# A layer's forward and backward pass on one core: turned weights prepared in the forward chain, loads at both phase changes queued in order of need, and a tail with its small blocks spread

## The chip, the core and the metric

The kernel runs on one core of a Trainium2 chip. The metric is device time in microseconds (us) of one execution; the profile is one execution of the same program under the hardware profiler. TensorE does the matmuls, VectorE and ScalarE empty its accumulators, GpSimd (POOL) copies, clears and issues DMAs, and SyncE (SP) issues DMAs only.

## The reference, cut to what matters

The output is a transformer layer and the gradients of everything in it.

```python
# A: attention with a recurrent memory of M = 8 rows, S = 2048 tokens, segments of 32 -> 64 steps one after another
mem = mem0
for s in range(64):
    h = concat([mem, layernorm(x)[32*s : 32*s+32]])      # 40 rows of D = 448
    q, k, v = h @ Wq, h @ Wk, h @ Wv                     # 16 heads of 256 -> 4096 columns
    o = softmax(mask(q k^T / 16)) v @ Wo
    mem, out[s] = o[:8], o[8:]
h  = x + out
# B: gated feed-forward unit (FFN), F = 1792
h2 = h + (silu(n @ w_gate) * (n @ w_up)) @ w_down        # n = layernorm(h)
# returned: h2 and, for the given gradient of h2, d x, d mem0, d Wq, d Wk, d Wv, d Wo, d w_gate, d w_up, d w_down
```

So there is a forward chain of 64 dependent segments, an FFN phase (forward and backward for 8 units of 256 rows), a backward chain of 64 segments, and a tail that computes all weight gradients.

## The kernel before

Between the phases the weights in on-chip memory are exchanged. The FFN backward needs w_gate, w_up and w_down turned (transposed), and the backward chain needs all four attention weights turned. Before, each is turned by a DMA transpose at the moment of the phase change. A helper does one weight in five DMAs; other weights take one transpose each:

```python
def transposed_rows(k, dst, src2d, tmp):
    for kc in range(3):
        nc.sync.dma_start_transpose(out=dst[:, kc, :], in_=src2d[:, kc * P:(kc + 1) * P])
    nc.sync.dma_start_transpose(out=tmp, in_=src2d[:, k.D - P:k.D])
    nc.sync.dma_start(out=dst[0:64, 3, :], in_=tmp[64:P, :])
    ...
# ffn_phase, one unit of two row tiles (cut)
for gi in range(NT // G):
    for tt in range(G):
        nc.sync.dma_start(out=h_t, in_=dr["Hh"][rows, :])
        nc.vector.tensor_scalar(out=hn_t[:, 0:D], in0=h_t, ...)                       # layernorm
        nc.sync.dma_start_transpose(out=hnT[:, :, tt * P:(tt + 1) * P], in_=hn_t)
        nc.sync.dma_start(out=dout_t[:, 0:D], in_=GO2[rows, :])
        nc.sync.dma_start_transpose(out=doT[:, :, tt * P:(tt + 1) * P], in_=dout_t)
    if gi == 0:
        transposed_rows(k, WdT_sb, Wd2, wdT_tmp)
        nc.gpsimd.dma_start(out=Wd_sb, in_=...)
        nc.sync.dma_start_transpose(out=WgT_sb, in_=Wg2)
        nc.sync.dma_start_transpose(out=WuT_sb, in_=Wu2)
    proj(Wg_sb, hnT, gate)                                                            # L560: the matmuls of proj
    ...                                                                               # L589: VectorE in gate
# backward_chain, ahead of its loop
transposed_rows(k, WoT_sb, k.Wo2, woT_tmp)
...
prep_tile(NT - 1)
load_seg(NSEG - 1)                                     # V, Q, K of the first segment, turned by DMA
for (Wsrc, WT) in ((k.Wk2, WkT_sb), (k.Wv2, WvT_sb), (k.Wq2, WqT_sb)):
    nc.sync.dma_start_transpose(out=WT, in_=Wsrc)      # L706
# one backward segment, the order in which it needs weights: WoT, then
heads("v", ...); rows_in("v", WvT_sb, 0, MC)           # heads: results go to blk[nm]; rows_in: L780
heads("k", ...); rows_in("k", WkT_sb, 0, 20)
heads("q", ...); rows_in("k", WkT_sb, 20, MC); rows_in("q", WqT_sb, 0, MC)
```

In the tail, each half of an attention weight gradient needs 16 row tiles (`X_`, by DMA transpose) and four packed blocks of memory rows (`M_`). The four blocks are loaded, copied and turned one after another through one load buffer and one pack buffer:

```python
def load_m(nm, hf):
    for g in range(NG):
        nc.gpsimd.dma_start(out=ld, in_=dr["M_" + nm]...)
        nc.vector.tensor_copy(out=pk[:, 0:8], in_=ld[...])       # L919
        nc.scalar.copy(out=pk[:, 8:16], in_=ld[...])
        ...
            nc.tensor.transpose(pt[...], pk[...], ident[:, :])   # L925
```

Of the kernel before, what the change touches and what calls it, by code (L numbers as in the profile page):

```python
# [9 lines left out]
FP32 = mybir.dt.float32  # L10
# [26 lines left out]
class _K:  # L37
# [31 lines left out]
    def evac(self, out, in_, eng=None):  # L69
        nc = self.nc  # L70
        if eng is None:
            eng = "v" if (self._evac_i % 2 == 0) else "s"
            self._evac_i += 1
        if eng == "v":
            nc.vector.tensor_copy(out=out, in_=in_)  # L75
        else:
            nc.scalar.copy(out=out, in_=in_)  # L77
# [69 lines left out]
def run_all(k: _K):  # L147
# [67 lines left out]
    for nm in ("q", "k", "v"):  # L215
        dr["X_" + nm] = dt("X_" + nm, [NT, P, MC * P])
        dr["M_" + nm] = dt("M_" + nm, [NT, P, MC * 32])
    k.dr = dr

    forward_chain(k)  # L220
    ffn_phase(k)
    backward_chain(k)
# [12 lines left out]


def transposed_rows(k, dst, src2d, tmp):

    nc = k.nc
    for kc in range(3):  # L240
        nc.sync.dma_start_transpose(out=dst[:, kc, :], in_=src2d[:, kc * P:(kc + 1) * P])
    nc.sync.dma_start_transpose(out=tmp, in_=src2d[:, k.D - P:k.D])
    nc.sync.dma_start(out=dst[0:64, 3, :], in_=tmp[64:P, :])
    nc.gpsimd.memset(dst[64:P, 3, :], 0.0)


def ln_bwd(k, outs, dxn_ap, xn_ap, rstd_col, t1, junk):
# [13 lines left out]
    for out_ap, resid_ap, c0, c1 in outs:  # L261
        nc.vector.scalar_tensor_tensor(out=out_ap, in0=t1[:, c0:c1], scalar=rstd_col, in1=resid_ap, op0=ALU.mult, op1=ALU.add)


def forward_chain(k: _K):
# [125 lines left out]
    def to_token_major(blk, t):  # L391
        for hf in range(2):
            ot = stg()
            nc.sync.dma_start_transpose(out=ot.rearrange("p (a b) -> p a b", b=P),
                                        in_=blk[:, 16 * hf:16 * hf + 16, :].rearrange("p c n -> p (c n)"))
            nc.gpsimd.dma_start(out=dr["X_o"][t][:, hf * 2048:(hf + 1) * 2048], in_=ot)

    for s in range(NSEG):
# [7 lines left out]
        with k.prio.crit():  # L406
            wpass(Wq_sb, s, qT)
            wpass(Wk_sb, s, kT)
            pS = k.ps1()
# [8 lines left out]
            for b in range(4):  # L418
                for kc in range(KC):
                    for g in range(2):  # L420
# [3 lines left out]
                                         start=(kc == 0), stop=(kc == KC - 1), skip_group_check=True)  # L424
            S_sb = k.f32("f2", 8 * L, "S_sb")[:].rearrange("p (h n) -> p h n", n=L)
# [33 lines left out]
            for j in range(MC):  # L459
                nc.tensor.matmul(pO[32 * (j % 4):32 * (j % 4) + M, 0:D], lhsT=o8[:, j, :], rhs=Wo_sb[:, cj(j), :],  # L460
                                 start=(j < 4), stop=(j >= MC - 4), skip_group_check=True)
            for (c0, n, v) in ov:
                k.evac(xblk[:, c0:c0 + n, r * SEG:(r + 1) * SEG], v[:, :, 0:SEG], "svs"[c0 // 12])
# [17 lines left out]
        if (r == 0 and t > 0) or s == 2:  # L481
            prep_tile(t + 2)
        if r == 3:
# [8 lines left out]
            to_token_major(xblk, t)  # L492
        if jm == 15:
            to_token_major(mblk, NT + s // 16)
# [4 lines left out]
            nc.gpsimd.dma_start(out=dr["XN"][r0:r0 + P, :], in_=mrow[:, 0:DP])  # L499


def ffn_phase(k: _K):
# [12 lines left out]
    Wg_sb, Wu_sb = W(0, KC, F), W(14, KC, F)  # L515
    dout_b = [W(28 + i, DP) for i in range(4)]
    WdT_sb, Wd_sb = W(32, KC, F), W(46, FC, D)
    wdT_tmp = W(58.25, F)
    WgT_sb, WuT_sb = W(64, FC, D), W(76.25, FC, D)
    big = [W(96 + 7 * i, G, FC, P) for i in range(4)] + [W(88.5, G, FC, P)] + [A(7 * i, G, FC, P) for i in range(6)]  # L520
    tstg_b = [A(42 + 3.5 * i, FC, P) for i in range(2)] + [W(58.25, FC, P)]
    hnT_b = [A(49 + 2 * i, KC, G * P) for i in range(2)]
    doT_b = [A(53 + 2 * i, KC, G * P) for i in range(2)]
    h_b = [A(57 + 0.875 * i, D) for i in range(4)]
    hn_b = [A(60.5 + i, DP) for i in range(4)]
    o_b = [B(0.875 * i, D) for i in range(2)]
    dhb_b = [B(2 + i, DP) for i in range(2)]
    junk = B(4, D)

    pad_rows(k, Wg_sb, Wg2, nc.gpsimd)  # L530
    pad_rows(k, Wu_sb, Wu2, nc.gpsimd)
    sd = smal.tile([P, NT], FP32, name="sd2", bufs=1)
    nc.scalar.activation(out=sd[:], in_=mv2[:, :, 1], func=ACT.Sqrt, bias=k.eps_t[:], scale=1.0)
    nc.vector.reciprocal(out=rstd2[:], in_=sd[:])
# [3 lines left out]
    for i in range(2):  # L538
        nc.gpsimd.memset(dhb_b[i][:, D:DP], 0.0)

# [7 lines left out]
    def tmajor(src, t, tt, dst):  # L548
        stg = tstg_b[rot[0] % 3]
# [14 lines left out]
    for gi in range(NT // G):  # L564
        hnT, doT = hnT_b[gi % 2], doT_b[gi % 2]
        for tt in range(G):
            t = G * gi + tt
            rows = slice(t * P, (t + 1) * P)
            h_t, hn_t, dout_t = h_b[t % 4], hn_b[t % 4], dout_b[t % 4]
            nc.sync.dma_start(out=h_t, in_=dr["Hh"][rows, :])  # L570
            nc.vector.tensor_scalar(out=hn_t[:, 0:D], in0=h_t, scalar1=mv2[:, t, 0:1], scalar2=rstd2[:, t:t + 1],
                                    op0=ALU.subtract, op1=ALU.mult)
            nc.sync.dma_start_transpose(out=hnT[:, :, tt * P:(tt + 1) * P], in_=hn_t)
            nc.gpsimd.dma_start(out=dr["HN"][rows, :], in_=hn_t[:, 0:D])
            nc.sync.dma_start(out=dout_t[:, 0:D], in_=GO2[rows, :])
            nc.sync.dma_start_transpose(out=doT[:, :, tt * P:(tt + 1) * P], in_=dout_t)
        if gi == 0:
            transposed_rows(k, WdT_sb, Wd2, wdT_tmp)
            nc.gpsimd.dma_start(out=Wd_sb, in_=Wd2.rearrange("(c p) d -> p c d", p=P))
            nc.sync.dma_start_transpose(out=WgT_sb, in_=Wg2)  # L580
            nc.sync.dma_start_transpose(out=WuT_sb, in_=Wu2)

        e = gi % 2
        g, z, t1, dz, u = big[5 + e], big[7 + e], big[9], (big[10], big[4])[e], big[0 + e]
        sg = big[2 + e]
# [15 lines left out]
        proj(Wu_sb, hnT, up)  # L601
        proj(WdT_sb, doT, dzf)
        for tt in range(G):
            t = G * gi + tt
            rows = slice(t * P, (t + 1) * P)
            tmajor(z, t, tt, dr["Zt"])
# [4 lines left out]
            nc.vector.tensor_tensor(out=o_t, in0=pf[:, 0:D], in1=h_b[t % 4], op=ALU.add)  # L611
            nc.gpsimd.dma_start(out=OUT0[rows, :], in_=o_t)
        for tt in range(G):
            nc.vector.tensor_tensor(out=u[:, tt], in0=dz[:, tt], in1=u[:, tt], op=ALU.mult)
            nc.vector.tensor_tensor(out=u[:, tt], in0=u[:, tt], in1=sg[:, tt], op=ALU.mult)
            nc.vector.tensor_tensor(out=g[:, tt], in0=dz[:, tt], in1=g[:, tt], op=ALU.mult)
        for tt in range(G):
            t = G * gi + tt
            rows = slice(t * P, (t + 1) * P)
            tmajor(u, t, tt, dr["DGP"])  # L620
            tmajor(g, t, tt, dr["DU"])
            pdh = k.fx1()
            i = 0
            for (srcT, WT) in ((u, WgT_sb), (g, WuT_sb)):
                for c in range(FC):
                    nc.tensor.matmul(pdh[:, 0:D], lhsT=srcT[:, tt, c, :], rhs=WT[:, c, :], start=(i == 0), stop=(i == 2 * FC - 1))
                    i += 1
            dh_t = k.f32("f3", D, "dh_t")
            t1f = k.f32("f2", D, "t1f")
            ln_bwd(k, [(dh_t[:], dout_b[t % 4][:, 0:D], 0, D)], pdh[:, 0:D], hn_b[t % 4][:, 0:D], rstd2[:, t:t + 1], t1f[:], junk)  # L630
            nc.gpsimd.dma_start(out=dr["DH"][rows, :], in_=dh_t[:])
            dh_b = dhb_b[tt]
            nc.scalar.copy(out=dh_b[:, 0:D], in_=dh_t[:])
# [432 lines left out]
```

## Time and profile before

The time is 3459.89 us (median of 3 runs, 3448.79 to 3468.05). The profiled execution is one of the shorter ones, 3429.5 us; a second profile of the same kernel, taken later, has 3438.8 us.

First the page: busy time of TensorE, then TensorE's busy tenths and its granted clock in 40 slices of 85.7 us.

```profile
PE 3044.6 (89%) x55036; PEld 2058.0 (60%) x55046; DVE 1308.3 (38%) x2912; ACT 971.0 (28%) x2171; POOL 616.2 (18%) x1293
...
PE   5999999999999578882999999999999899999999
...
PEclk8999999999999899995999999999999899999999
```

TensorE is at nine tenths almost everywhere. The slices that are not are the load at the start, the change to the FFN (slices 14 and 15), the FFN, the change to the backward chain (slice 19, with clock 0.5), and slice 32, where the tail begins. That is where time can be won without removing matmuls.

The view of TensorE's waits (what was waited for, sum in us, times, longest) names them:

```profile
PE psf L560 <- DMA arA<-arA: 48.6, 6, 43.7
PE psf L737 <- POOL arA L672: 41.1, 1, 41.1
...
PE psf L560 <- DVE arA L589: 27.8, 7, 7.2
PE po L780 <- DMA arW<-in_A_Wv_dram: 25.5, 1, 25.5
...
PE ph L925 <- DVE arA L919: 15.5, 11, 6.5
PE psf L385 <- issue: 13.1, 16, 2.1
```

The first is the change to the FFN (the first rows come turned), the second and fourth are the change to the backward chain, the third is inside the FFN, the fifth the packed memory blocks of the tail. L385, "issue", is in the forward chain.

The timeline of SyncE's queue (start, duration, what) shows why the two changes are slow: transposes of whole weights stand one behind another in the queue.

```profile
1157.27 12.55 SPq L241 DMA_TRANSPOSE arW<-in_B_w_down_dram  x2
...
1179.62 15.34 SPq L580 DMA_TRANSPOSE arW<-in_B_w_gate_dram  x1
...
1552.21 21.00 SPq L706 DMA_TRANSPOSE arW<-in_A_Wq_dram  x1
...
1587.86 16.90 SPq L706 DMA_TRANSPOSE arW<-in_A_Wk_dram  x1
1604.85 13.64 SPq L706 DMA_TRANSPOSE arW<-in_A_Wv_dram  x1
```

Note that the scheduler issued Wq first, although the program names Wk, Wv, Wq and the segment needs Wv first.

### The profile page before, as it was taken

How to read it: one execution, taken by the hardware profiler on the slowest of the kernel's cores; microseconds unless marked ns; L12 is line 12 of the kernel's file. 1: busy time of each engine (PE TensorE's matmuls, PEld its weight loads, DVE VectorE, ACT ScalarE, POOL GpSimd, SP SyncE). 2: the span in 40 equal slices, each digit the busy share in tenths (PEclk: the TensorE clock that was granted, in tenths of full speed). 3: DMA queues.
4: the chain of work that ended last, by engine and by line, in shares of the span. 5: the costliest groups of instructions: out<-in, count | busy, mean ns of one | idle time of the engine just before them, and what ended most of it. 6: DMA issues, size and time to landing. Idle time of an engine off the chain costs nothing.

```text
span 3429.5 us, 120857 instructions
## 1 busy us (share of the span) xinstructions
PE 3044.6 (89%) x55036; PEld 2058.0 (60%) x55046; DVE 1308.3 (38%) x2912; ACT 971.0 (28%) x2171; POOL 616.2 (18%) x1293
## 2 busy tenths in 40 slices
PE   5999999999999578882999999999999899999999
PEld 4777777777777355661666666666666454443444
DVE  4444444444444256670444444444444201111101
ACT  1333333333333223330333333333333202111100
POOL 2111111111111111111122121212221111111111
PEclk8999999999999899995999999999999899999999
DMA  7545433644544787899688777878787969888571
GB/s 263 155 133 149 155 125 128 174 136 131 148 139 134 196 189 176 185 210 229 142 159 178 164 168 157 177 161 165 166 177 163 308 195 209 175 173 173 155 249 38
DMA packets 994213, 583.65 MB, mean 170 GB/s; under 512 B 904564, under 2 KB 913108, under 8 KB 992100
## 3 DMA queue, kind: packets, MB, share of 16 engines
q1 hardware_dynamic: 925748, 340.37, 47.6%
q0 software_dynamic: 67952, 235.56, 20.6%
q8 instruction: 430, 7.05, 0.9%
q14 instruction: 83, 0.68, 0.1%
HBM read 104.05 MB, written 250.19 MB: 103 GB/s over the span
## 4 chain that ended last, share of the span: by engine, by line
PE 61%; issue 13%; DMA 10%; DVE 8%; SPq 4%; ACT 2%; POOL 2%; ACTq 0%; DVEq 0%; POOLq 0%
PE psf L385 12%; PE po L780 7%; PE psf L422 5%; PE psf L737 5%; PE psf L945 4%; PE psf L715 4%; PE po L460 3%; PE fx L486 3%; PE fx L839 3%; PE psf L560 2%; SPq L910 2%; PE psf L802 2%; DVE arA L75 2%; PE psf L469 2%; DMA arW<-in_A_Wo_dram 2%
## 5 line engine op out<-in xcount | busy, mean ns | idle before, releaser
L77 ACT CAST arA<-psf 128x320 bf16<-128x320 f32 (+4 forms) x1139 | 487.0, 447 | 1611.8 <-PE psf L385 449.5
L75 DVE CAST arA<-psf 128x384 bf16<-128x384 f32 (+6 forms) x1029 | 491.7, 495 | 1085.1 <-PE psf L945 363.3
L385 PE MATMUL psf<-arA,arW 128*128 128x40 bf16 x16384 | 434.9, 181 | 34.3 <-issue 13.1
L385 PEld LDWEIGHTS <-arW 128*128 128x128 bf16 x16384 | 432.7, 97 | 49.6 <-issue 26.9
L780 PE MATMUL po<-arW,arA 128*32 128x448 bf16 x6144 | 355.2, 362 | 46.9 <-DMA arW<-in_A_Wv_dram 25.5
L737 PE MATMUL psf<-arA,arW 128*128 128x40 bf16 x8192 | 219.6, 180 | 51.3 <-POOL arA L672 41.1
L945 PE MATMUL psf<-arW,arA 128*128 128x512 bf16 x990 | 252.7, 383 | 13.4 <-DMA arW<-X_k 7.1
L422 PE MATMUL psf<-arW,arA 128*64 128x512 bf16 x2048 | 260.5, 383 | 2.4 <-DMA arW<-in_A_Wv_dram 2.4
L737 PEld LDWEIGHTS <-arW 128*128 128x128 bf16 x8192 | 215.3, 96 | 71.1 <-issue 70.6
L780 PEld LDWEIGHTS <-arA 128*32 128x32 bf16 x6144 | 155.2, 98 | 163.1 <-issue 35.2
L945 PEld LDWEIGHTS <-arA 128*128 128x128 bf16 x1440 | 135.4, 98 | 189.3 <-issue 44.7
L560 PE MATMUL psf<-arA,arW 128*128 128x256 bf16 x1344 | 166.1, 286 | 82.3 <-DMA arA<-arA 48.6
L560 PEld LDWEIGHTS <-arW 128*128 128x128 bf16 x1344 | 137.3, 102 | 113.5 <-issue 85.8
L422 PEld LDWEIGHTS <-arA 128*64 128x64 bf16 x2048 | 147.2, 111 | 70.3 <-issue 3.5
L75 DVE CAST arB<-psf 40x320 bf16<-40x320 f32 x320 | 107.7, 336 | 98.7 <-PE psf L451 65.0
L715 PEld LDWEIGHTS <-arW 128*128 128x128 bf16 x2048 | 87.9, 101 | 66.4 <-issue 62.7
L77 ACT CAST arB<-psf 128x96 bf16<-128x96 f32 (+1 forms) x320 | 98.2, 307 | 104.2 <-DVE arB L75 51.7
L486 PE MATMUL fx<-arW,arA 128*128 128x448 bf16 x512 | 124.5, 353 | 0.0
L747 ACT COPY arA<-psf 128x1024 bf16<-128x1024 bf16 x128 | 123.4, 1015 | 3.2 <-PE psf L746 1.7
L460 PE MATMUL po<-arW,arB 128*8 128x448 bf16 x2048 | 110.8, 359 | 9.0 <-DMA arW<-in_A_Wo_dram 5.4
L715 PE MATMUL psf<-arB,arW 128*128 128x80 bf16 x2048 | 98.7, 203 | 17.3 <-DVE arB L764 7.7
L966 PE MATMUL psf<-arW 128*128 128x448 bf16 x450 | 95.4, 361 | 5.8 <-DMA arW<-X_o 5.7
(238 smaller groups left out, 3741.8 us busy)
## 6 DMA issues: line engine op xcount, KB each, us to landing
QT<-arA POOLq DMA_DIRECT2D x64, 512.0 KB, 4.1
KT<-arA SPq DMA_DIRECT2D x64, 512.0 KB, 3.4
VG<-arA SPq DMA_DIRECT2D x64, 512.0 KB, 3.1
X_o<-arA POOLq DMA_DIRECT2D x40, 512.0 KB, 4.3
X_v<-arA POOLq DMA_DIRECT2D x32, 512.0 KB, 6.5
X_k<-arA POOLq DMA_DIRECT2D x32, 512.0 KB, 4.0
X_q<-arA POOLq DMA_DIRECT2D x32, 512.0 KB, 4.3
arW<-X_o SPq DMA_DIRECT2D x30, 512.0 KB, 13.7
```

The lines of the kernel that those rows point to most:

```text
L75: nc.vector.tensor_copy(out=out, in_=in_)
L77: nc.scalar.copy(out=out, in_=in_)
L385: nc.tensor.matmul(pss[b][:, jj * L:(jj + 1) * L], lhsT=W_sb[:, kc, c * P:(c + 1) * P], rhs=hT_roll[:, kc, sl, :], start=(kc == 0), stop=( ...
L422: nc.tensor.matmul(pV[b][64 * g:64 * g + 64, 0:512], lhsT=hT_flat[:, kc, sl * L:sl * L + 64], rhs=Wv_sb[:, kc, n * 512:(n + 1) * 512], sta ...
L460: nc.tensor.matmul(pO[32 * (j % 4):32 * (j % 4) + M, 0:D], lhsT=o8[:, j, :], rhs=Wo_sb[:, cj(j), :], start=(j < 4), stop=(j >= MC - 4), sk ...
L486: nc.tensor.matmul(px[:, 0:D], lhsT=xblk[:, j, :], rhs=Wo_sb[:, cj(j), :], start=(j == 0), stop=(j == MC - 1))
L560: nc.tensor.matmul(ps[:, f2 * 256:(f2 + 1) * 256], lhsT=Wt[:, kc, c * P:(c + 1) * P], rhs=xT[:, kc, :], start=(kc == 0), stop=(kc == KC - 1))
L715: nc.tensor.matmul(ps[b][:, i * 2 * L:(i + 1) * 2 * L], lhsT=lhs[:, cl, :], rhs=rhs_bd[:, cl // 2, :, :].rearrange("p g n -> p (g n)"), st ...
L737: nc.tensor.matmul(pss[b][:, jj * L:(jj + 1) * L], lhsT=WoT_sb[:, kc, c * P:(c + 1) * P], rhs=do_roll[:, kc, sl, :], start=(kc == 0), stop ...
L747: nc.scalar.copy(out=dO_sb[:, 8 * hf:8 * hf + 8, :], in_=ph.rearrange("p (c n) -> p c n", n=P))
L780: nc.tensor.matmul(pH[32 * (j % 4):32 * (j % 4) + 32, 0:D], lhsT=blk[nm][:, j, r * SEG:(r + 1) * SEG], rhs=WT[:, cj(j), :], start=(nm == " ...
L945: nc.tensor.matmul(pa[2 * kc + g][:, 0:w], lhsT=lhs_of(b)[:, kc * P:(kc + 1) * P], rhs=rhs_of(b, g), start=(b == 0), stop=(b == nblk - 1), ...
```

## The change

The intent has four parts.

1. In the forward chain, where the DMA engines are half idle, 44 pieces of weight are turned by DMA, staged on chip and stored to seven new DRAM tensors `Tq, Tk, Tv, To, Td, Tg, Tu`.
2. At the phase changes those tensors come back by plain loads in SyncE's queue, placed where the memory comes free, in order of need. TensorE itself turns the first FFN rows, and the last unit's u and g.
3. FFN buffers are doubled (two dh buffers) and the last two units change places; the backward chain is a generator that the last FFN unit calls, so that its loads start inside the FFN.
4. In the tail, the packed memory blocks are loaded and packed one group ahead, spread between groups of matmuls, and the w_gate and w_up gradients stand between attention halves.

The diff, cut to its core (cuts are marked `...`):

```diff
+    for nm in ("q", "k", "v"):
+        dr["T" + nm] = dt("T" + nm, [P, MC, D])
+    ...                                                # To, Td, Tg, Tu
+    k.fl = _FFNLoads(k)
     forward_chain(k)
-    ffn_phase(k)
-    backward_chain(k)
+    back = backward_chain(k)
+    ffn_phase(k, lambda: next(back, None))
+    for _ in back:
+        pass
...
# forward_chain
+    def piece():
+        if not pieces:
+            return
+        nm, Ws, i0, n = pieces.pop(0)
+        T, ot = dr["T" + nm], stg()
+        ...
+            nc.sync.dma_start_transpose(out=o3, in_=Ws[:, i0:i0 + n])
+            nc.gpsimd.dma_start(out=T[:, i0 // P:i0 // P + m, :], in_=o3)
...
             wpass(Wq_sb, s, qT)
+            if s == NSEG - 1:
+                k.fl.at(0)                             # w_gate, w_up over the memory of Wq
             wpass(Wk_sb, s, kT)
+            if s == NSEG - 1:
+                k.fl.at(1)                             # rows of the first unit
...
-            for j in range(MC):                        # the memory product ...
+            if s + 1 < NSEG:                           # ... not for the last segment
+                for j in range(MC):
...
+        if r < 3 and s >= 4:
+            piece()
...
# ffn_phase
+    def tmajor_pe(src, t, tt, dst, i):
+        stg = A(3.5 * i, F)                            # i = 0..3: A(0 .. 14 KB)
+        ...                                            # 14 transposes on TensorE, evictions into stg
+        nc.gpsimd.dma_start(out=dst[t * P:(t + 1) * P, :], in_=stg)
...
-    for gi in range(NT // G):
+    for n, gi in enumerate(list(range(last - 1)) + [last, last - 1]):
+        if n > 0:
+            load_in(n, gi)                             # rows of this unit, in SyncE's queue
+        if n == last:
+            back()
         for tt in range(G):
+            for src, dst in ((hn_t, hnT), (dout_t, doT)):
+                if n == 0:
+                    ...                                # TensorE turns the rows of the first unit
+                else:
+                    nc.sync.dma_start_transpose(out=dst[...], in_=src)
...
# backward_chain
-    for (Wsrc, WT) in ((k.Wk2, WkT_sb), (k.Wv2, WvT_sb), (k.Wq2, WqT_sb)):
-        nc.sync.dma_start_transpose(out=WT, in_=Wsrc)
+    yield                                              # called in the last unit
+    nc.sync.dma_start(out=WoT_sb[:, 0:3, :], in_=dr["To"][:, 0:3, :])
+    ...
+    yield
+    v_in = load_v(NSEG - 1)
+    with tc.issue_after(v_in.ins):
+        nc.sync.dma_start(out=WvT_sb, in_=dr["Tv"])
+    yield
+    nc.sync.dma_start(out=WkT_sb, in_=dr["Tk"])
+    nc.sync.dma_start(out=WqT_sb, in_=dr["Tq"])
...
# tail_phase
-    ld = A(33.5, 4, 16, 32)
-    pk = A(37.5, 16, 4, 32)
+    ld_b = [A(33.5, 4, 16, 32), B(0, 4, 16, 32)]
+    pk_b = [A(37.5, 16, 4, 32), B(4, 16, 4, 32)]
...
+                (f0, p0, t0), (f1, p1, t1), (f2, p2, t2), (f3, p3, t3) = mem    # fetch, pack, turn of each group
+                at = {0: [p0, f2], 4: [lambda: t0(xt[NT]), p1, f3], 8: [lambda: t1(xt[NT + 1]), p2],
+                      12: [lambda: t2(xt[NT + 2]), p3], 16: [lambda: t3(xt[NT + 3])]}
...
+        if hi == 0:
+            ...
+            up_grad("DGP", 7, mems[1])
+        if hi == 2:
+            up_grad("DU", 8, mems[3])
```

## The prediction

> **What bounds the kernel now.** The page shows TensorE 89% busy, clock 0.96. In 50 us windows the forward chain (100 to 1150 us), the backward chain (1650 to 2650) and most of the tail have TensorE busy 46 to 48 of 50 us; transfers cannot speed those up. The time to win is in four places.
>
> 1. *Forward to FFN.* The waits show one 43.7 us TensorE idle (1165.8 to 1209.5) ended by the DMA transpose of the first rows. In the SyncE timeline, weight transposes of 5.0, 12.6, 2.7 and 15.3 us stand before it.
> 2. *FFN.* Eight units in 331 us hold 291 us of TensorE work. The waits: 27.8 us on VectorE in the gate. VectorE stands waiting for the DH store of the single dh buffer (3.8 to 6.3 us per unit in the chain).
> 3. *FFN to backward.* TensorE ends at 1540.6; the first segment waits 41.1 us, behind 21.0 us of Wq transpose, then 25.5 us for WvT. The second starts at 1629.3; later ones take 15.7 us, so 73 us are lost.
> 4. *Tail.* Waits from 2700 us: 15.5 us for packed memory blocks, about 15 for X tiles. After a 6.5 us wait eight transposes take 1.03 instead of 0.61 us. The Trainium skill, "TensorE: Matmul & The Clock Gate", Part 1, says an idle array falls to half clock for some microseconds; the clock row agrees (0.70 and 0.57 at the phase changes).
>
> **Costs of the change.**
> - 44 weight pieces are transposed and stored in the forward chain. DMA is about 0.45 busy there and SyncE mostly waits for evictions: +6 us (0 to +15).
> - Phase change 1: plain loads start when each weight's last pass ends; TensorE turns the first rows (16 transposes, 2 us). 9.5 MB at the 420 GB/s of the initial weight loads is 23 us, overlapped. The wait falls to 3-6 us; the dropped memory product saves 1.7: -41 us.
> - FFN: two dh buffers remove most of the 27.8 us, and weight transposes no longer delay the first units: -20 us (-8 to -28).
> - Phase change 2: Wo and Wv arrive inside the last unit. Only Wk and Wq, 7.3 MB, 18 to 22 us, start after the last dh; needed about 11 and 16 us into the segment, they leave waits of 10 to 18 us together: -58 us (-45 to -65). Turning the last u and g on TensorE: 56 transposes, +4 us.
> - Tail: packing a group ahead and FFN gradients between attention halves: -20 us (-10 to -27).
>
> Sum -129 us. All of it is TensorE idle on the chain, so it should come through almost whole.
>
> **Predicted: 3330 us, 8 in 10 between 3290 and 3372; faster by over 2% 0.95, same 0.04, slower 0.01.**
>
> **Right or wrong in the profile.** TensorE busy time about unchanged (3040 to 3060 us), share near 92%. The waits of 43.7, 41.1 and 25.5 us gone; in their place single waits under 8 us on turned weights. FFN about 310 us from first gate to last dh. Forward segments still 17.1 us. No wait over 3 us on packed memory blocks.
>
> **What would make it wrong.** Pieces stand in SyncE's queue before row transposes or the stores of K and V and stretch the forward segments: 1 us each would cost 60 us. Loads collide at a phase change, so that a weight is late by tens of us. The scheduler places the variance of the last tiles ahead of the first rows.[...]

The clocks of 0.70 and 0.57 are those of the windows from 1150 to 1200 and from 1550 to 1600 us; the clock row's slices there show 0.8 and 0.5.

## More of the kernel before

`blk[nm]`, the on-chip block that collects the results of four segments, is one of five buffers of 8 KB per partition: `blk_b[(3 * tb + i) % 5]` for i = 0, 1, 2 (v, k, q), where tb counts groups of four segments.

## The result, and the profile after

| kernel | median us | lowest to highest | fast runs |
|---|---|---|---|
| before | 3454.92 | 3448.79 to 3468.05 | 4 |
| after | 3350.77 | 3338.81 to 3359.87 | 4 |

The ratio is 0.9692, with a 95% interval from 0.9646 to 0.9737: faster by 3.1%, or 104 us. Every ratio here is the mean time of one kernel's fast runs over that of the kernel before in the same rounds, so it is not quite the ratio of the medians quoted beside it. The total lies in the predicted range, 21 us above the centre.

The page's lines after, as shown of before (slices of 83.6 us):

```profile
PE 3034.4 (91%) x55076; PEld 2059.1 (62%) x55086; DVE 1310.2 (39%) x2919; ACT 974.4 (29%) x2178; POOL 644.7 (19%) x1344
...
PE   5899999999999969995999999999999889999998
...
PEclk8999999999999989997999999999999999999999
```

The waits after:

```profile
PE po L903 <- DVE arA L75: 42.1, 16, 23.3
...
PE psf L650 <- DMA arW<-arW: 31.9, 5, 20.6
PE psf L427 <- issue: 21.3, 27, 3.2
...
PE psf L650 <- DVE arA L689: 4.4, 2, 4.2
```

The waits of 43.7, 41.1 and 25.5 us are gone, that on VectorE in the gate fell from 27.8 to 4.4, and the packed memory blocks have left the list. But there are two new waits of over 20 us: one in the FFN (L650) and one at the second phase change (L903). The issue waits of the forward chain have grown from 13.1 to 21.3 us at their main line.

To see each part separately I cut every trace at the same events: VectorE's first copy of memory rows, then TensorE's last product of the forward chain, first gate product, last product of the FFN, start of the second backward segment, first weight-gradient product, end. The pieces add up to the span, in us:

| phase | before, two profiles | after, two profiles | difference of means | predicted |
|---|---|---|---|---|
| head | 57.8, 58.1 | 57.3, 58.8 | 0 | 0 |
| forward chain | 1107.9, 1104.0 | 1127.3, 1121.5 | +18 | +6 |
| change to FFN | 43.7, 47.1 | 1.9, 1.9 | -44 | -41 |
| FFN | 331.1, 342.6 | 328.4, 332.6 | -6 | -20 |
| change to backward, with the first segment | 88.7, 85.7 | 61.6, 58.3 | -27 | -58 + 4 |
| backward chain | 1084.0, 1075.6 | 1082.8, 1085.6 | +4 | 0 |
| tail | 716.2, 725.8 | 685.1, 682.2 | -37 | -20 |
| span | 3429.5, 3438.8 | 3344.4, 3341.0 | -91 | -129 |

The same pieces differ by up to 11.5 us between two profiles of one kernel, so single microseconds mean nothing here. Both profiles of the kernel before lie below most of its timed runs, so this table shows 91 us where the timed runs show 104. The second profile of each comes from a rerun of the unchanged file:

> The changed kernel once more, as the yardstick for the other runs of this call and to see how far its parts scatter. Expected: ratio to before 0.965 to 0.974; forward chain (first to last copy of the memory rows) 1104 us as in the first profile if its lengthening is real, near 1086 us if it was chance; one wait of about 20 us in the second FFN unit and one of about 23 us in the first backward segment.

Measured: 3345.14 us (4 runs) beside 3456.63 (7 runs), ratio 0.9696, interval 0.9649 to 0.9743. From its first to its last copy the forward chain takes 1100.1 us (1086.4 and 1081.8 in the two profiles of the kernel before), so its lengthening is real; the two long waits come again, with 22.4 and 24.3 us.

> The kernel before, profiled once more, since its first profile (3431 us) is 20 to 35 us below its timed runs. Expected: 3440 to 3465 us, with the surplus in the forward chain or in the FFN to backward change; the tail within 3 us of 716 us.

Measured: 3440.57 us (1 run, state unknown) beside 3450.56 (7 runs). Its pieces are in the table. The time is as expected, but the surplus is in the FFN and in the tail (725.8 us, 9.6 over the first profile), not where I had looked for it.

The first phase change did what was intended. TensorE's timeline there:

```profile
1179.71 4.89 PE L564 MATMUL fx<-arW,arA 128*128 128x448 bf16 x24
1184.44 1.06 PE L679 MATMUL psf<-ident,arW 128*128 128x128 bf16 x16
1186.50 3.76 PE L650 MATMUL psf<-arW 128*128 128x256 bf16 x33 [1.01 <-DVE arW L75]
```

The last forward product runs straight into 16 transposes (1.06 us), and after 1.01 us of eviction the first gate product starts. The other parts need experiments.

### The profile page after: what moved, and what is told of

Read it like the earlier page. It is cut to its first block, busy times and chain, and to the rows that moved or that the text cites. A ratio compares the mean times of both kernels' runs of the same rounds, so it can differ in the third digit from the quotient of the medians.

```text
span 3344.4 us, 121108 instructions
## 1 busy us (share of the span) xinstructions
PE 3034.4 (91%) x55076; PEld 2059.1 (62%) x55086; DVE 1310.2 (39%) x2919; ACT 974.4 (29%) x2178; POOL 644.7 (19%) x1344
## 3 DMA queue, kind: packets, MB, share of 16 engines
q8 instruction: 431, 7.06, 0.9%
## 4 chain that ended last, share of the span: by engine, by line
PE 71%; DVE 10%; issue 9%; DMA 7%; ACT 2%; POOL 1%; SPq 1%; ACTq 0%; DVEq 0%; POOLq 0%
PE psf L427 13%; PE psf L1074 8%; PE po L903 7%; PE psf L494 6%; PE psf L860 5%; PE psf L837 4%; PE po L535 3%; PE fx L564 3%; PE psf L1095 3%; PE fx L962 3%; PE psf L650 2%; DVE arA L75 2%; PE fx L731 2%; PE fx L1079 2%; PE psf L925 2%
## 5 line engine op out<-in xcount | busy, mean ns | idle before, releaser
L427 PE MATMUL psf<-arA,arW 128*128 128x40 bf16 x16384 | 436.4, 181 | 41.8 <-issue 21.3
L427 PEld LDWEIGHTS <-arW 128*128 128x128 bf16 x16384 | 433.3, 97 | 58.1 <-issue 36.4
L903 PE MATMUL po<-arW,arA 128*32 128x448 bf16 x6144 | 353.2, 360 | 46.1 <-DVE arA L75 42.1
L1074 PE MATMUL psf<-arW,arA 128*128 128x512 bf16 x1030 | 259.5, 379 | 0.0
L903 PEld LDWEIGHTS <-arA 128*32 128x32 bf16 x6144 | 153.5, 97 | 160.8 <-DVE arA L75 44.9
L860 PEld LDWEIGHTS <-arW 128*128 128x128 bf16 x8192 | 214.2, 96 | 32.0 <-issue 31.9
L650 PE MATMUL psf<-arW 128*128 128x256 bf16 x1344 | 156.3, 276 | 42.6 <-DMA arW<-arW 31.9
L650 PEld LDWEIGHTS <-arW 128*128 128x128 bf16 x1344 | 133.0, 99 | 68.3 <-issue 34.8
L837 PEld LDWEIGHTS <-arW 128*128 128x128 bf16 x2048 | 87.7, 100 | 72.9 <-issue 69.8
L1095 PEld LDWEIGHTS <-arW 128*128 128x128 bf16 x606 | 59.5, 100 | 74.9 <-DMA arW<-X_o 14.5
```

Source lines behind the costliest of these rows:

```text
L427: nc.tensor.matmul(pss[b][:, jj * L:(jj + 1) * L], lhsT=W_sb[:, kc, c * P:(c + 1) * P], rhs=hT_roll[:, kc, sl, :], start=(kc == 0), stop=( ...
L650: nc.tensor.matmul(ps[:, f2 * 256:(f2 + 1) * 256], lhsT=Wt[:, kc, c * P:(c + 1) * P], rhs=xT[:, kc, :], start=(kc == 0), stop=(kc == KC - 1))
L837: nc.tensor.matmul(ps[b][:, i * 2 * L:(i + 1) * 2 * L], lhsT=lhs[:, cl, :], rhs=rhs_bd[:, cl // 2, :, :].rearrange("p g n -> p (g n)"), st ...
L860: nc.tensor.matmul(pss[b][:, jj * L:(jj + 1) * L], lhsT=WoT_sb[:, kc, c * P:(c + 1) * P], rhs=do_roll[:, kc, sl, :], start=(kc == 0), stop ...
L903: nc.tensor.matmul(pH[32 * (j % 4):32 * (j % 4) + 32, 0:D], lhsT=blk[nm][:, j, r * SEG:(r + 1) * SEG], rhs=WT[:, cj(j), :], start=(nm == " ...
L1074: nc.tensor.matmul(pa[2 * kc + g][:, 0:w], lhsT=lhs_of(b)[:, kc * P:(kc + 1) * P], rhs=rhs_of(b, g), start=(b == 0), stop=(b == nblk - 1), ...
```

## Experiments

### The change to the backward chain: what is the 23.3 us wait?

TensorE's product at L903 waits for an eviction by VectorE, which is not slow: it waited itself. From the timelines of the changed kernel, start and duration first, idle time before it and its releaser in brackets:

```profile
1540.21 0.20 POOL L826 MEMSET arB<- 128x128 f32 x1 [16.87 <-DMA DHb<-arB]
...
1540.93 0.54 POOL L636 DMA_DIRECT2D DGP<-arA  x1
...
1551.54 0.56 DVE L75 CAST arA<-psf 128x384 bf16<-128x384 f32 x1 [23.54 <-DMA DGP<-arA]
...
1555.85 0.62 ACT L76 CAST arA<-psf 128x384 bf16<-128x384 f32 x2 [26.69 <-DMA DU<-arA]
```

VectorE and ScalarE wait to write `blk["v"]` until the stores of the turned u and g have landed. Those stores read `A(0 .. 14 KB)`, the staging of `tmajor_pe`; `blk_b[0]` and `blk_b[1]`, which the first segment fills with v and k, are `A(0 .. 16 KB)`. POOL issues the stores late, because ahead of them stands a memset that waits 16.87 us for a store of another buffer. My theory: the overlap makes the wait. The rival: the segment waits for its weights anyway, and the eviction is only the last to be ready. Shifting the ring of five buffers by two gives the first segment `blk_b[2..4]` and leaves every transfer as it is.

```diff
-        blk = {nm: blk_b[(3 * tb + i) % 5] for i, nm in enumerate("vkq")}
+        blk = {nm: blk_b[(3 * tb + i + 2) % 5] for i, nm in enumerate("vkq")}
```

> One line: the ring of five backward blocks starts two places later, so that the first segment's blocks no longer lie on the memory from which the last FFN unit's turned u and g are stored. Theory (the wait of 23 us in the first backward segment is for those stores, which stand behind others in the GpSimd queue and behind the weights): the evictions wait for no store any more, the time from the last dh product to the second backward segment falls from 61.6 us to about 50 us, and the whole kernel gains 8 to 14 us against the changed kernel. Rival (it is really the late Wv that the segment waits for): the wait turns into one on the turned Wv of about the same length, and the gain is under 4 us.

Measured: 3332.73 us (3322.78 to 3334.63), ratio 0.9636 (0.9595 to 0.9678), beside 3345.14 (3340.76 to 3369.22) of the changed kernel in the same rounds: the ranges don't overlap. The piece fell from 61.6 and 58.3 to 48.4 us. The waits at this place, in this run:

```profile
PE po L903 <- DMA arW<-Tk: 12.3, 1, 12.3
PE po L903 <- DMA arW<-Tv: 7.4, 1, 7.4
```

The wait on the eviction is gone, and half of it has come back as waits on weights. So both were right in part: the overlap cost some 12 us, and behind it the weights were late. In this trace Tq is issued before Tk, as in the changed kernel, although the program names Tk first, and the segment needs Tk earlier. The next run fixes that order too:

```diff
-    nc.sync.dma_start(out=WkT_sb, in_=dr["Tk"])
-    nc.sync.dma_start(out=WqT_sb, in_=dr["Tq"])
+    k_in = nc.sync.dma_start(out=WkT_sb, in_=dr["Tk"])
+    with tc.issue_after(k_in.ins):
+        nc.sync.dma_start(out=WqT_sb, in_=dr["Tq"])
```

> As e1_blk_shift, and the turned Wk is issued before the turned Wq (the scheduler had placed Wq first, though Wk is needed about 5 us earlier). Theory: Wk lands about 10 us earlier and the two loads still end at the same time, so the wait on Wk goes and a shorter one on Wq stays: from the last dh product to the second segment 42 to 48 us, 3 to 8 us less than e1_blk_shift. Rival (the transfers as a whole set the end, order does not matter): within 2 us of e1_blk_shift.

Measured: 3336.66 us (3334.61 to 3339.73), ratio 0.9658 (0.9625 to 0.9691): no better than with the shift alone. The piece is 45.9 us. The waits became 7.4 us on Tv, 1.4 on Tk and 8.0 on Tq. They ended at 1537.5, 1546.6 and 1557.7 us: 3.67 MB about every 10 us, some 363 GB/s for the weights alone. Over the 45 us from 1515 us the changed kernel moved 15.93 MB, 354 GB/s, but that mean hides two rates. The windows view of the changed kernel (the last three numbers are the granted clock, the DMA share and GB/s):

```profile
1500.00:1525.00 25.00, 21.35 (x272) 14.12 (x269) 17.00 (x30) 6.67 (x10) 8.93 (x13) 1.00 0.98 256
1525.00:1550.00 25.00, 2.44 (x50) 2.21 (x50) 0.49 (x1) 0.80 (x1) 3.38 (x7) 0.50 1.01 434
```

The DMA share is about one in both. While DMA transposes stand beside the load of To they move 256 GB/s; with the plain loads of the three weights and a few stores they move 434 (432 in this run). The Trainium skill, "DMA: Bandwidth & Descriptors", Specifications, states about 358 GB/s as the limit of a core's share of the HBM and 435 GB/s as the ceiling of the fabric; for this program, which runs on one core, the 434 lie well above the first and at the second. Changing the order moves the waits, because the transfers themselves are what is short.

Can the loads start earlier? In the changed kernel SyncE's queue holds Tv back:

```profile
1502.93 9.25 SPq L641 DMA_TRANSPOSE arW<-arA  x1
1512.29 6.04 SPq L641 DMA_TRANSPOSE arB<-arA  x1
1518.44 2.42 SPq L784 DMA_TRANSPOSE arA<-VG  x1
1520.97 0.53 SPq L820 DMA_DIRECT2D arW<-Tv  x1
```

The transposes of z in the last unit (L641), which run beside the load of To, keep the queue for 15 us, and the last FFN product ended at about 1515 us, before Tv was issued. The run "e7_all" (below, because it also has the cure of the FFN) turns that z on TensorE.

### The FFN: a wait that had not been there

The VectorE waits went as predicted, but the second unit waits 20.6 us for its turned rows. SyncE's queue after the first phase change:

```profile
1191.88 17.00 SPq L437 DMA_TRANSPOSE arA<-arA  x2
1208.93 0.57 SPq L279 DMA_DIRECT2D arW<-Hh  x1
...
1216.66 10.26 SPq L437 DMA_TRANSPOSE arA<-arA  x2
...
1229.92 0.43 SPq L279 DMA_DIRECT2D arW<-Hh  x1
...
1231.76 2.07 SPq L682 DMA_TRANSPOSE arW<-arW  x1
```

The output blocks of the forward chain (L437), which nothing waits for, are turned in this queue while the weight loads run, and take 17.00 and 10.26 us for two each, where two took 4.83 and 6.39 us in the kernel before. The rows of the second unit (L279) and their transposes (L682) stand behind them. The experiment loads those rows with those of the first unit and lets TensorE turn them too:

```diff
         elif place == 1:
             self.load_in(0, 0)
+            self.load_in(1, 1)
...
-        if n > 0:
+        if n > 1:
             load_in(n, gi)
...
-                if n == 0:
+                if n <= 1:                             # TensorE turns the rows
```

> The second FFN unit gets the treatment of the first: its h and grad_out rows are loaded together with those of the first unit, and TensorE turns its rows. Theory (the 20.6 us wait at the start of the second unit is the order of the SyncE queue: its row loads and DMA transposes stand behind the transposes of the attention output blocks, 17.0 and 10.3 us, and of z and u): the wait falls below 3 us, first gate to last dh goes from 328 to about 309 us, and the kernel gains 15 to 20 us against the changed kernel. Rival (DMA is saturated there and something else would be late instead): a wait of 10 us or more appears on a weight or a store, and the gain is under 8 us.

Measured: 3342.99 us (3336.85 to 3352.68), ratio 0.9678 (0.9641 to 0.9715); not told apart from the changed kernel in time. In the trace the 20.6 us wait is gone and the FFN takes 321.2 us instead of 328.4 and 332.6. The waits on turned rows still add up to this, though:

```profile
PE psf L651 <- DMA arW<-arW: 16.9, 4, 8.0
```

The theory of the queue's order holds for the second unit. The cure gives only about 9 us of the FFN, because these other waits stay: in the changed kernel the fourth, fifth, sixth and eighth unit together wait 11.3 us for turned rows (the rest of the 31.9 us), here 16.9, of which 8.0 are in the fourth. One sees the size of what is lost here: 321.2 less 16.9 is 304 us, near the predicted 310.

### Both cures, and the last unit's z turned by TensorE

```diff
# with the edits of the two runs above:
+        if n < last:
+            prep(n + 1)                # next unit's loads and transposes, queued before this unit's z
...
-            tmajor(z, t, tt, dr["Zt"], n == last)
+            if n == last:
+                tmajor_pe(z, t, tt, dr["Zt"], None, tstg_b[1 + tt].rearrange("p f n -> p (f n)"))
+            else:
+                tmajor(z, t, tt, dr["Zt"])
```

> All that the runs pointed to, in one kernel: blocks of the first backward segment off the memory of the turned u and g; Wk before Wq; the last unit's z turned by TensorE, so that no DMA transposes stand before Wv in the SyncE queue; the second FFN unit's rows loaded with the first's and turned by TensorE; later units' rows loaded and turned one unit ahead. Theory: last dh to second backward segment 34 to 42 us (Wv issued about 12 us earlier), first gate to last dh 308 to 316 us, together 25 to 35 us less than the changed kernel: ratio to before about 0.960 to 0.963. Rival (the transfers at both phase changes are bound by the DMA engines' rate, so earlier issue moves nothing): 46 us or more at the second change and a gain under 18 us.

Measured: 3332.09 us (3328.52 to 3342.04), ratio 0.9673 (0.9641 to 0.9705). The FFN is 321.1 us, where 308 to 316 had been expected, and waits on turned rows are still 19.0 us, so turning one unit ahead gave nothing. The second phase change is 49.4, where 34 to 42 had been expected. The weights now are late like this:

```profile
PE po L917 <- DMA arW<-Tv: 7.7, 1, 7.7
PE po L917 <- DMA arW<-Tq: 6.1, 1, 6.1
PE psf L874 <- DMA arW<-To: 6.1, 2, 3.5
PE po L917 <- DMA arW<-Tk: 3.4, 1, 3.4
```

Four weights wait where three did, for 23.3 us together: the FFN ended earlier, and To is late too. The theory wanted no DMA transpose in SyncE's queue ahead of Tv; it did not come to that. The place of z was taken by the transpose of the first segment's V, which program order puts before Tv:

```profile
1500.64 13.97 SPq L797 DMA_TRANSPOSE arA<-VG  x1
1514.91 0.34 SPq L833 DMA_DIRECT2D arW<-Tv  x1
```

Tv was issued 10.5 us after the last FFN product, 6.0 us in the changed kernel. So this run does not test an earlier start. This run has three edits and does not improve on the one-line shift, whose ratio 0.9636 (0.9595 to 0.9678) is the best of the kernels with right results; the intervals overlap. The DMA engines are busy through this change (share 1.01 at 379 GB/s over the 50 us from 1499 us), so the transfers, the slow transposes among them, are the limit; fewer bytes, or memory that comes free earlier, is what I would try next. The Trainium skill, "DMA: Bandwidth & Descriptors", "Issuing engines are not separate DMA queues", says that transfers run on the same 16 engines whoever issues them and interleave. No run here tests that, since SyncE issues all four weights; what the runs show is that one weight gains what another loses.

### The forward chain: what do the pieces cost, and how?

The prediction allowed 6 us. Below, for each kernel, are TensorE's waits named "issue" and the line of the windows view, in a window from about the thirteenth segment to the end of the chain; the last numbers of that line are the granted clock, the DMA share and GB/s. The kernel before:

```profile
PE psf L385 <- issue: 9.5, 13, 1.8
...
290.00:1165.00 875.00, 819.68 (x20013) 635.37 (x20012) 367.58 (x838) 274.43 (x600) 135.93 (x310) 0.99 0.47 143
```

The changed kernel:

```profile
PE psf L427 <- issue: 12.6, 19, 3.2
PE psf L486 <- issue: 5.8, 7, 1.8
...
290.00:1184.00 894.00, 830.53 (x20101) 640.62 (x20102) 373.08 (x851) 279.19 (x611) 157.61 (x354) 0.98 0.62 178
```

DMA share goes from 0.47 to 0.62, TensorE's "issue" waits at these lines from 9.5 (10.6 with a second line) to 18.4 us. No wait on SyncE's queue or on a store appears, which was what I had feared. Two runs tell what it is about the pieces. Both compute wrong weights (and so wrong gradients), with the same sizes and types. The first makes no pieces: seven plain copies from DRAM to DRAM, from segment 4 on, fill the T tensors.

```diff
+    del pieces[:]
+    jobs = [(dr["Td"], gate, None), ...]              # seven, one for each T tensor
     def piece():
-        nm, Ws, i0, n = pieces.pop(0)
-        ...                                           # transpose to staging, store
+        T, rows_of, cols_of = jobs.pop(0)
+        nc.gpsimd.dma_start(out=T..., in_=...)        # plain copy, not turned
```

> Wrong result on purpose: the 44 weight pieces of the forward chain are left out; seven plain copies early in the chain fill the seven turned weights with other numbers of the same size. Theory (the pieces are what lengthens the forward chain): first to last copy of the memory rows falls from 1100 to 1105 us back to 1084 to 1090 us, TensorE's idle put down to nothing the profile shows (issue) on the Q, K and score products falls from about 25 us to about 10 us, and the kernel gains 12 to 18 us against the changed kernel. Rival (chance, or another part of the change): unchanged within 4 us.

Measured: 3329.82 us (3316.94 to 3336.99), ratio 0.9634 (0.9601 to 0.9668). The lines of this run:

```profile
PE psf L427 <- issue: 7.6, 13, 1.4
...
300.00:1178.00 878.00, 824.00 (x20074) 636.97 (x20071) 371.83 (x850) 277.97 (x609) 137.50 (x315) 0.99 0.46 144
```

From segment 12 to the last the chain takes 865.9 us, in the kernel before 870.9 and 867.9, in the changed one 882.0 and 881.9 (worked out from the records of the copies that begin each segment). So the pieces make all of this 13 us. The seven big copies themselves slow the first twelve segments, so the whole forward chain, 1120.1 us, does not show it (from first to last copy 1097.4 us, not the expected 1084 to 1090). The second run keeps every piece, its place, its staging and its store, but loads it plainly instead of turning it:

```diff
-            nc.sync.dma_start_transpose(out=o3, in_=Ws[:, i0:i0 + n])
+            Wp = k.aps["B_w_down"] if nm in "gu" else k.Wo2
+            nc.sync.dma_start(out=o3, in_=Wp[i0:i0 + n, :].rearrange("(c p) d -> p c d", p=P))
```

> Wrong result on purpose: every piece keeps its place in the SyncE queue, its staging buffer, its bytes and its store, but its DMA transposes become plain loads of other rows of the same size. Theory (DMA transposes keep all 16 engines busy with small packets, so that TensorE's instruction fetches come late): the forward chain falls back to within 5 us of the run without pieces, with issue waits near 10 us. Rival (the pieces' places in the SyncE and GpSimd queues and the staging buffers cost the time, or simply the bytes): the chain stays at 1100 us or more.

Measured: 3354.73 us (3339.57 to 3360.67), ratio 0.9716 (0.9682 to 0.9751). From segment 12 on: 882.9 us, issue waits 17.8 us (L427 and L488), DMA share 0.57 at 177 GB/s. The same cost without one transpose of a weight: the rival, that it is the transposes with their many small packets, falls. What is left is that the bytes (143 to 178 GB/s), the stores, or the pieces' places in the queues and staging buffers cost it; I did not separate those.

How bytes that nobody waits for delay TensorE can be read from the records, and this is a correlation, not an experiment. In the forward chain there are 8 issue gaps of 0.5 us or more before and 18 after, 8.0 and 20.2 us together (7 and 18 in the second profiles). Each of these 26 ends 1.2 to 1.9 us after a packet of the profile's DMA queue named "instruction" has landed; at evenly spaced moments that distance has a median of 2.8 us. So TensorE's own instructions seem to come late when the DMA engines are busier. Those 26 packets did not take longer than others (median 0.93 us, of all 1.02 to 1.05), so they would have to start late; why is open. The page's list of DMA queues has them as traffic of their own, the same before and after (packets, MB, share of 16 engines):

```profile
q8 instruction: 430, 7.05, 0.9%
...
q8 instruction: 431, 7.06, 0.9%
```

Of the 13 us from segment 12 on, the issue waits make 9.9 (10.8 and 9.2 us before, 19.8 and 19.9 after). The granted clock adds nothing there: 0.986 and 0.988 in the two profiles before, and the same after; the 0.99 and 0.98 of the views above differ by their windows. TensorE's busy time is 2.6 us longer, for which I have no reason. Half-clock stretches do follow some of the gaps. The Trainium skill, "TensorE: Matmul & The Clock Gate", Part 1, says that an array idle for about 3.4 us falls to half clock; here a gap of 1.68 us that ended at 140.9 us was followed, from 142.4 us, by a half-clock stretch of 6.8 us.

### The tail: which of its two changes won the time, and what it is worth

One run keeps the memory blocks spread, but takes the FFN gradients out from between the attention halves and puts them back behind:

```diff
-        att(hi, mems[hi], mems[hi + 1] if hi not in (0, 2) else None)
-        if hi == 0:
+        att(hi, mems[hi], mems[hi + 1])
+        if hi == 1:
             nc.gpsimd.dma_start(out=HN[:, 0:NT, :], in_=...)
-            up_grad("DGP", 7, mems[1])
-        if hi == 2:
-            up_grad("DU", 8, mems[3])
+    up_grad("DGP", 7, None)
+    up_grad("DU", 8, None)
```

> The changed kernel, its tail put back in one respect: the two FFN gradients come after all six attention halves again, as before; the memory blocks stay spread between groups of token blocks. Theory A (the spreading of the memory blocks is what takes the tail's waits away): tail 685 to 692 us against 682 to 685, no wait over 1 us on packed memory blocks. Theory B (the FFN gradients between the halves give the transposed loads of the next half time to arrive): waits on X tiles come back, 10 to 20 us together, tail 695 to 710 us.

Measured: 3351.34 us (3349.68 to 3357.2), ratio 0.9723 (0.9689 to 0.9757). The tail takes 680.9 us, as in the changed kernel (685.1, 682.2), and no wait on memory blocks or attention tiles comes back. So spreading the blocks, with the second load and pack buffer that goes with it, is the whole gain; the FFN gradients between the halves give nothing that can be seen.

The other run puts the whole old tail behind the changed phases. It was run twice, the second time with more rounds:

```diff
# tail_phase: as in the kernel before; all else as in the changed kernel
```

> The changed kernel with the whole tail of before (memory blocks packed at the end of a half, FFN gradients last). Theory: the tail change is worth its full 31 to 34 us by itself: from the first Wo gradient product to the end about 716 us as before, against 682 to 685 us. Rival (part of the gain comes from transfers that the earlier phases left in a better state): 695 to 708 us.

Measured: 3443.29 us (1 run, state unknown) beside 3450.56; the tail takes 767.1 us.

> The changed kernel with the whole old tail once more, now timed, because the single look gave a tail of 767 us where the kernel before has 716 and 726 us. Expected if that look was a bad execution: tail 716 to 730 us, time 3375 to 3390 us. Expected if the old tail really is slower behind the changed phases: tail 750 us or more again, time 3420 us or more, and waits on packed memory blocks of 30 us or more together.

Measured: 3419.94 us (3412.9 to 3431.29, 4 runs), ratio 0.9927 (0.989 to 0.9964); the tail takes 756.5 us. In TensorE's waits from 2700 us on, the packed blocks:

```profile
PE ph L1048 <- DVE arA L1042: 38.8, 12, 11.1
```

This surprised me. I had expected the old tail to take here what it takes in the kernel before, 716 to 726 us, and it took 30 to 50 us more: the wait on packed blocks is 38.8 us instead of 15.5 and 22.2. The code of the tail is the same. Its DMAs are slower: the transposes of the X tiles of k and q take 5.9 to 6.1 us by their medians in place of 5.0 to 5.5, and the slowest load of a packed k block 9.9 and 10.9 us in place of 6.0 and 7.5. What differs is what ran before, and seven more tensors in DRAM. The last run declares only these tensors in the kernel before, and touches each once with a one-row copy at the start, so that they are not dropped:

```diff
+    for nm in ("q", "k", "v"):
+        dr["T" + nm] = dt("T" + nm, [P, MC, D])
+    ...                                               # To, Td, Tg, Tu, as in the changed kernel
...
+    for nm in ("q", "k", "v", "o", "d", "g", "u"):
+        nc.gpsimd.dma_start(out=dr["T" + nm][0:1, 0, 0:D], in_=X2[0:1, :])
```

> The kernel before, unchanged but for the seven DRAM tensors of the changed kernel (the turned weights), declared in the same place and each touched by one copy of one row at the start. It asks why the old tail takes 757 to 767 us behind the changed phases and only 716 to 726 us in the kernel before. If the extra tensors shift the tail's buffers in DRAM and that slows its transfers (X transposes 5.9 instead of 5.0 to 5.3 us, the slowest landing of a packed-memory load 9 to 11 instead of 5 to 7.5 us), this kernel's tail takes 745 us or more and the whole is 25 us or more slower than before (ratio 1.007 or more). If placement is not the cause, the tail stays at 716 to 726 us and the ratio within 0.997 to 1.003; then the cause lies in what the changed phases do, and stays open.

Measured: 3501.35 us (3478.51 to 3514.54) beside 3457.89 (3436.9 to 3480.37), ratio 1.0114 (1.0042 to 1.0185). The tail takes 748.6 us. Its wait on packed blocks:

```profile
PE ph L933 <- DVE arA L927: 32.9, 12, 6.6
```

The medians of the X transposes of k and q into the larger area are 6.3 and 6.0 us and the slowest load of a packed k block 9.9, as in the mixed kernel. So in this profile unused tensors in DRAM, with the tail's code untouched, slow the tail's transfers by most of what the mixed kernel shows: 23 to 32 us of 31 to 51. Only the tail of this run should be read: its seven copies hold up the memsets in POOL's queue at the start (the head takes 73.3 us in place of 58), and the first phase change took 65.0 us, with two transposes of w_down at 30.3 us in place of 12.6, which I cannot explain. The ratio is therefore not the price of the tensors. It is one profile, but two of the mixed kernel agree with it. The runs were on different chips, and on this one the kernel before was only timed (3436.9 to 3480.37 us, elsewhere 3440.22 to 3469.87), not profiled. What it is about the addresses is open; the profile does not show them.

So the comparison of the changed tail with the old one in its own kernel (-37 us) mixes two things: behind the changed phases the old tail loses 31 to 51 us, 23 to 32 of them with the new tensors alone, and the new tail gains 71 to 85 us over that (756.5 and 767.1 less 685.1 and 682.2). One block ahead is enough to make the slower loads invisible.

## Why the prediction was right or wrong

The total, 3330 us with a range of 3290 to 3372, held: 3350.77. Its main claim was right: waits at the phase changes were on the critical path and their removal comes through. TensorE's busy time, predicted 3040 to 3060, is 3034.4, the share 91%. But it is a sum in which several terms were mis-sized and partly cancel: 17 us more than said in the tail stand against 12, 14 and 27 us less in three other parts. That the total fell in the range is partly luck.

- **Change to FFN, -41: right.** The waits shrank from 43.7 and 47.1 us to 1.9, as the step said, by plain loads and TensorE's transposes. The order of the variance, named as a risk, was as wanted.
- **Forward chain, +6: wrong size; measured +18.** The step was "DMA is about 0.45 busy there and SyncE mostly waits for evictions". Both are true, and no wait on SyncE's queue appears. The cost is mostly TensorE's issue gaps, at a DMA share of 0.62. A mean share below one does not say that transfers are free. The segment's median rose from 17.2 and 17.1 to 17.4 and 17.3 us; some segments take 1 to 5 us more. That all of it comes from the pieces is shown for the stretch from segment 12; the late fetch of instructions is only argued.
- **FFN, -20: mechanism right, the sum wrong; measured -6.** The waits on VectorE fell from 27.8 to 4.4 us, and VectorE's own waits for the DH store, 33.2 us in 7 waits before, are gone; no run changes the dh buffers alone. The step "weight transposes no longer delay the first units" overlooked what else was in that queue: the output blocks' transposes, beside the very loads that had been moved earlier, delayed the second unit by 20.6 us; later units wait 11.3 us more for turned rows, against 4.9 for all units but the first before.
- **Change to backward, -58 + 4: measured -27.** The step that failed is "Wo and Wv arrive inside the last unit. Only Wk and Wq ... start after the last dh". Tv was issued after the last FFN product, behind z's transposes in SyncE's queue; so 11 MB, not 7.3, came after it. The second thing missed is that the staging of u and g overlaps the first segment's blocks, with stores that POOL issues late: taking that away alone won some 12 us. The rest is transfer time: the engines are full, and in two runs better orders only moved the waits. My rate of 420 GB/s was a peak of slices in the first loads, whose mean from 5 to 55 us is 354. For all bytes it was right once the plain loads ran (434); but the weights got about 363 of it, beside stores, and before them transposes kept the full engines at 256.
- **Tail, -20: measured -37; the right cause, the wrong half of the change and the wrong reference.** No wait over 3 us on packed blocks is left, as said. The gain comes from spreading the blocks alone. That the old tail gets slower behind the changed phases, by the new tensors for the most part as far as one run shows, was not foreseen at all; against it, the spreading is worth 71 to 85 us. TensorE's clock also gains. In the windows view the whole tail (2713 to 3429 us before, 2659 to 3344 after) has TensorE busy 670.72 us at clock 0.98 before, and 660.84 at 0.99 after, for the same products.
- **"Single waits under 8 us on turned weights": wrong for what stood in their place.** No wait on a turned weight is in the list, but one of 23.3 us on an eviction that waited for stores, and one of 20.6 us on rows.

The risks named ("loads collide at a phase change", "pieces stretch the forward segments") were the ones that came; their sizes were 10 to 30 us each.

## What to carry to other kernels

When loads are moved earlier, list everything else that shares their queue and their memory at that moment: here a transpose that nobody needed delayed the unit that was needed, and a staging buffer under the next phase's first output cost 12 us, which one line of index arithmetic won back. Cost transfers at the mean rate of a long stretch, with everything else that moves in it, transposes above all; and once the transfers are the limit, don't spend effort on their order. When an old part runs slower in a new kernel, compare the transfer times of the same tiles first; and prefer structures that fetch one block ahead, because they hide such shifts.

## What the Trainium skill lacked or had wrong

- Placement in DRAM: no page that I read says that declaring further tensors can slow the transfers of others. In one run with seven more tensors the tail took 748.6 us in place of 716.2 and 725.8, and its waits on packed blocks 32.9 us in place of 15.5 and 22.2. It would belong to "DMA: Bandwidth & Descriptors", whose "Latency and other measured facts" has a row on row pitches; the pitches did not change here.
- Instruction fetch: "Runtime: NRT & Kernel Launch", "Instruction fetch mechanics", describes how the engines' instructions are streamed in blocks of 16 KiB and calls the cost of a block boundary mostly hidden; it does not speak of this traffic as competing with data. The trace shows 431 packets of 16 KiB, 7.06 MB, in the "instruction" queue. All 26 issue gaps of 0.5 us or more in the forward chains of two traces end 1.2 to 1.9 us after a packet of the "instruction" queue landed, and there were 8 of them at a DMA share of about 0.45 and 18 at about 0.63. So up to 20.2 us are not hidden here, if this correlation is the cause.
- DMA transposes beside plain loads: "DMA: Bandwidth & Descriptors" gives a rate for transposes (261 GB/s in one kernel) ("Latency and other measured facts") but not how much they stretch. The transposes of two output blocks held SyncE's queue for 4.83 us in the kernel before and 17.00 us beside the weight loads of the changed one; a weight of 3.67 MB held it for 13.64 to 21.00 us, which is 269 to 175 GB/s.
- "TensorE: Matmul & The Clock Gate", Part 1, gives about 3.4 us of idleness before the half clock; it mentions frequent shorter idling too, without a length. Behind one issue gap of 1.68 us the trace shows a half-clock stretch of 6.8 us.
- "DMA: Bandwidth & Descriptors", Specifications, lists about 358 GB/s as the limit of a core's share of the HBM. The row divides what two cores share, so it is no limit for this program on one core, and that is no error of the page: 10.85 MB in 25 us at the second phase change are 434 GB/s. The mean of 354 GB/s over 45 us there only looks like the limit, because it holds slow transposes.
